# Masks of one head pair applied by VectorE instead of TensorE, with a new order of the first half, in an attention-and-MLP kernel

## Chip, cores and metric

The kernel runs on one core of a Trainium2 chip. The metric is the device time of one execution in microseconds (us), the median of several runs.

## What is computed

Attention over 4 batches, 8 heads, 768 tokens and 64 columns a head, followed by a two-layer MLP over all 3,072 tokens:

```python
scores = scale * np.matmul(q, k.transpose(0, 1, 3, 2))
stream_keep = causal & (is_sink | in_win)
mask = np.where(retr, causal, stream_keep)
scores = np.where(mask, scores, -1e9)
a = softmax(scores)
x = (a @ v), heads side by side            # 3072 x 512
h = x @ w_in                               # 512 x 2048
g = np.maximum(h, 0) + alpha * np.minimum(h, 0)
out = g @ w_out                            # 2048 x 512
```

Heads 0, 2 and 6 are "retrieval" heads with a causal mask. Heads 1, 3, 4, 5 and 7 are "streaming" heads: a token sees the first 4 tokens (sinks) and the last 64.

## The kernel before

**Segments.** The work of attention is cut into 16 segments n, four a batch. A segment is a pair of heads: (2, 6), (1, 5), (0, 4), (3, 7). Segment 3 is the fourth pair of batch 0; both of its heads are streaming. Inputs are read in fp32 into rings of four buffers each (`qf`, `kf`, `vf`), cast to bf16, transposed on TensorE (PE) for the first eight segments and by DMA later, and multiplied to scores with keys on the partitions. ScalarE (ACT) takes the exponential out of PSUM into `eR` (retrieval heads, 2 buffers) or `eS` (streaming heads, 3 buffers). A matmul with the values and a column of ones gives outputs and row sums; VectorE (DVE) divides. The result is transposed into `xT`, the MLP's input.

**Masks, two ways.** For n < 4 the mask is added on PE before the exponential: after each score matmul a second matmul of the identity with a constant of 0 and -30000 (`nmr` causal, `nms` and `nms6` streaming) goes into the same PSUM columns (lines 459 and 498). For n >= 4 the mask is multiplied in after the exponential: DVE multiplies the bf16 result by a constant of 0 and 1 (`mr`, `ms`, `ms5`; lines 476 and 527).

**MLP.** It runs in 8 pieces t of 512 or 256 tokens. `P{t}.{f}` are the matmuls with w_in (line 598), ACT takes relu(-h) (`p`, line 603), DVE makes g from it (`g`, line 610), `O{t}.{s}.{u}` are the matmuls with w_out (line 618), ACT copies the result (`o`) and POOL's or SP's queue stores it. The piece P0.f is cut in three parts (pairs 0 and 1, pair 2, pair 3) for f < 6, so that it can start before pair 3 is ready. Weights are loaded by POOL's queue with a cast: `wi0`..`wi7` for w_in (wi0 and wi1 serve columns 0 to 511, i.e. f 0 to 3; wi2 and wi3 f 4 to 7; wi4 and wi5 f 8 to 11; wi6 and wi7 f 12 to 15) and `wo0`..`wo3` for w_out (wo u serves quarter u of each O).

**The order.** All of it is one list of names, `ORDER`, written out (lines 14 to 71). Each engine gets its own instructions in the order in which their names stand in the list, and works through them one by one; waits between engines follow from the data. The names:

- `Lq n`, `Lk n`, `Lv n`: loads, issued by SP's queue (part of Lk0 and `La`, the slopes, by ACT's). A load into a ring slot waits until the slot's last reader is done. SP's loads take turns on 8 semaphores.
- `Cq n`, `Ck n.h`, `Cv n`: casts, by POOL for n <= 5 (Cq0.0 DVE, Ck0.0 ACT), by DVE later (Cq6 and Cq7 by ACT). Cv also copies the sink rows of streaming heads on POOL (line 310).
- `Tq`, `Tk`: transposes on PE; `tq` copies the result out on ACT (tq0.1 on DVE); `tk` on DVE for n < 4, on ACT later.
- `S n.h.m`: scores; `s`: exponential (ACT); `m`: mask product (DVE); `A n.h`: output matmul, `a`: its division (DVE); `X n`: transpose of the output, `x`: copy into `xT` (DVE).
- `kz, vz, sz, qz, ro, so, vo`: constants set by DVE (kz2 by ACT, kz3 by POOL); `ms`, `mr`: the 0/1 masks, made by DVE; `nms`, `nmr`: made by POOL; `warm`: filler matmuls.

PSUM has eight banks. For n < 4 scores take a pair of banks out of two pairs (0, 1) and (2, 3), transposes bank 4 or 5, outputs bank 6 or 7; later all take any bank. From n = 4 on, scores are collected and issued in a group; a group with at least 576 columns in each head is issued with the two heads on the two halves of the array (line 427), another one on the whole array (line 420).

The pieces of code that choose the way of masking:

```python
# line 495, scores of a streaming head before the late segments
                one_score(n, hh, m, sc[:, x, o:o + w], kt[:, 128 * j:128 * (j + 1)],
                          qt[:, 124 * j:124 * j + w], n >= 4)
                if n < 4:
                    nc.tensor.matmul(sc[:, x, o:o + w], ident, (nms6 if j == 6 else nms)[:, 0:w],
                                     start=False, stop=True)
# line 787, in the list of items
                if n >= 4:
                    item(f"m{n}.{hh}.{m}", M_retr if RETR[h] else M_stream, n, hh, m)
```

The functions concerned: `M_retr` (470), `M_stream` (523), `S_retr` (442), `S_stream` (483), `thirds` (480: for n < 4, m = 0 covers two thirds of 384 columns, m = 1 the last third), `emit_burst` (414), `load_w_in` (704), `cast_v` (345), `factors` (659).

Of the kernel before, what the change touches and what calls it, by code (L numbers as in the profile page):

```python
# [14 lines left out]
Lq0.0 zero La id qz nmr Lk0 kz1 sz2 kz2 Ck0.1 vo Lk1 nms Ck0.0 qz0 Lq0.1 Lq1 kz0 Cq0.0 warm0 Tq0.0 warm1 sz1 tq0.0 Lq2  # L15
vz0 Cq0.1 Tk0.0 warm2 tk0.0 Lk2 S0.0.0 sz0 s0.0.0 Tk0.1 S0.0.2 Lv0 vz1 Cq1 s0.0.2 Lk3 tk0.1 Tq0.1 S0.0.1 Ck1.0 s0.0.1
Tq1 Ck1.1 vz2 Ck2.0 Tk1 ro Cq2 tq1 tq0.1 vz3 S0.1.1 S0.1.2 Ck2.1 s0.1.1 S0.1.0 Tk2 tk1.0 Cv0 tk1.1 s0.1.2 S1.1.1 Tq2
s1.1.1 so Ck3.1 A0.0 Lv1 s0.1.0 S1.0.1 tk2.1 S1.1.0 tq2 idf tk2.0 kz3 Lv2 Ck3.0 Lq3 A0.1 Cv1 s1.0.1 wi0 m6.0.2 s1.1.0
a0.0 S1.0.0 Tk3 S2.0.2 wi1 s1.0.0 Lv3 Cq3 a0.1 Lk4 X0 tk3.0 s2.0.2 wi2 Cv2 A1.0 S2.1.0 s2.1.0 x0 A1.1 a1.0 Cv3 S2.1.1
a1.1 Tq3 s2.1.1 S2.0.1 Ck4.0 X1 tk3.1 Lq5 tq3 S2.0.0 Ck4.1 A2.1 Lk5 mr m4.0.2 s2.0.1 s2.0.0 S3.1.0 x1 A2.0 S3.1.1  # L20
s3.1.0 a2.1 s3.1.1 S3.0.0 wi3 A3.1 wi4 s3.0.0 S3.0.1 s3.0.1 a2.0 Lk6 Tk4 Lq6 X2 a3.1 x2 A3.0 P0.3.0 tk4.0 P0.2.0 Al
a3.0 X3 Ck5.0 Cq5 x3 P0.0.0 tk4.1 wi5 wi7 P0.0.1 P0.2.1 P0.3.1 P0.1.0 Tq5 al Lq4 wi6 P0.2.2 P0.1.1 Lq7 P0.3.2 P0.1.2
P1.0 ms P0.0.2 p0.3 P0.5.0 P1.6 g0.3 tq5 Ck6.1 p0.1 P1.4 P0.5.1 Ck5.1 P0.5.2 p0.0 g0.0 Lk7 g0.1 p1.6 g1.6 p0.2 P0.6
P0.4.0 Tk5 Lv5 p0.5 wo0 g0.2 one P0.4.1 g0.5 p1.0 p1.4 Cq4 g1.0 p0.6 P0.11 Ck6.0 Lq8 P0.4.2 P1.2 g0.6 wo2 tk5.0 nr
tk5.1 nz0 g1.4 p1.2 Tq4 P1.8 m10.0.2 P0.10 S5.1.2 g1.2 wo1 p1.8 kfz0 p0.4 g1.8 Lk8 kfz1 wo3 p0.11 P0.14 g0.4 Cq6 P0.13
tq4 p0.14 kfz3 p0.10 P0.9 P0.8 g0.11 p0.13 g0.14 Tq6 p0.9 g0.10 g0.13 P1.10 g0.9 P0.12 tq6 p0.8 g0.8 Cq7 p0.12 P0.7
p1.10 P1.14 S5.1.1 p0.7 s5.1.2 g0.12 O0.0.0 S4.1.1 S4.1.4 Lv4 p1.14 Lq9 S4.0.0 g1.10 s5.1.1 S5.0.0 g0.7 g1.14 S4.0.1
kfz2 s4.0.0 s4.1.1 P0.15 s4.0.1 m4.0.0 Ck7.1 m5.1.1 P1.12 m4.1.1 s4.1.4 S4.0.4 S5.1.0 p0.15 g0.15 s5.0.0 S4.1.3 S4.0.2
O0.0.1 s4.1.3 s4.0.2 S5.0.2 S4.1.2 Tk6 Cv5 m5.1.2 p1.12 O0.1.0 Cv4 s5.0.2 m4.1.3 Lk9 m5.0.0 Cq8 Ck7.0 O0.1.1 O0.1.2
s4.0.4 s4.1.2 tk6.1 tk6.0 s5.1.0 Ck8 m4.0.4 O0.0.2 S4.1.5 S4.0.5 S4.0.3 S4.1.0 S6.1.2 m5.0.2 m4.1.4 s4.0.3 s4.1.0  # L30
s4.1.5 m5.1.0 O0.1.3 s6.1.2 g1.12 m4.0.1 Tq7 S5.0.1 O0.0.3 A5.1 s4.0.5 O0.3.0 O0.3.1 o0.0 Tk7 m4.0.3 m4.1.5 a5.1
s5.0.1 m4.0.5 m4.1.0 tk7.0 O0.3.2 A4.0 m5.0.1 o0.1 A4.1 tk7.1 Lv6 a4.0 Dk8.1 Dq8 tq7 a4.1 O0.3.3 o0.3 A5.0 a5.0 Lv7
S6.0.5 S6.1.1 S7.1.1 S6.0.4 S6.1.0 S7.0.0 s7.0.0 Cq9 Cv6 s6.1.0 O1.1.0 s6.0.4 s6.1.1 S7.0.1 S6.0.3 X5 nz1 O0.2.0
m6.0.4 s6.0.5 s7.0.1 S7.1.2 S6.0.1 x5 O1.1.1 s6.0.1 Ck9 s7.1.1 O1.1.2 S6.0.2 S8.1.0 m6.0.1 s7.1.2 S7.1.0 m7.0.0 s6.0.3
S7.0.2 S6.0.0 m6.1.2 S8.1.5 O0.2.1 O0.2.2 Dq9 m6.1.1 m6.0.3 Dk9.0 s6.0.2 m7.0.1 m7.1.1 s6.0.0 s7.1.0 Dk8.0 m6.1.0
m6.0.5 s7.0.2 m7.0.2 Cv7 m6.0.0 A6.1 O0.2.3 A6.0 O1.1.3 m7.1.2 Dk9.1 ns s8.1.0 m7.1.0 Lk10 o0.2 Lq13 o1.1 a6.0 A7.1
A7.0 O1.0.0 Lv8 a6.1 S8.1.4 s8.1.4 O1.0.1 s8.1.5 S8.0.0 S8.0.3 S9.1.0 S8.1.1 a7.0 S8.1.3 a7.1 S9.0.1 Lk11 Lk12 S9.0.0
O1.0.2 s8.0.0 Ck10 X6 s8.1.3 s8.0.3 s9.0.0 s8.1.1 Lv9 Lq10 s9.0.1 m8.0.0 X4 s9.1.0 O1.0.3 X7 S8.0.1 S8.0.4 x4 S9.0.2
# [24 lines left out]
A15.0 p5.0 a15.0 p5.4 O4.1.1 g5.8 O4.0.0 a14.0 m4.1.2 O4.2.0 g5.4 X15 P5.10 O4.1.2 O4.0.1 O4.2.1 m8.0.2 x15 X14 O4.0.2
P6.8 P6.6 O4.0.3 p5.10 g5.0 P6.1 O4.3.3 O4.2.2 g5.10 P6.7 p6.8 o4.0 p6.7 p6.6 P7.6 g6.7 g6.8 O4.2.3 P6.10 O4.1.3 P6.3
p6.10 o4.3 g6.10 P7.4 o4.2 O5.1.0 O5.1.1 P7.0 p6.1 g6.6 P6.2 g6.1 p6.3 O5.0.0 g6.3 o4.1 P6.13 p6.13 P7.14 g6.13 O5.0.1
p6.2 p7.0 P6.0 g6.2 O5.1.2 P6.5 g7.0 P6.11 p6.0 g6.0 O5.0.2 p6.11 O5.1.3 p7.4 p6.5 g6.11 P7.10 p7.14 m8.1.2 o5.1 g6.5
m12.1.2 P6.9 P6.4 g7.4 p6.9 g6.9 p6.4 O5.0.3 g7.14 P7.2 O6.1.0 P6.15 g6.4 p7.2 P7.12 p6.15 O6.1.1 O6.1.2 g7.2 o5.0
O6.0.0 g6.15 P6.14 P6.12 O6.0.1 p6.14 O7.0.0 O6.0.2 g6.14 p7.6 p7.12 p6.12 g6.12 g7.6 O6.3.0 O6.2.0 O6.2.1 O6.0.3 P7.8
O6.2.2 O6.1.3 g7.12 O6.3.1 p7.8 o6.1 p7.10 O6.3.2 O6.3.3 g7.8 O7.0.1 o6.3 g7.10 o6.0 L0 O6.2.3 O7.0.2 o6.2 O7.0.3 L1
l0 L2 o7.0 l1 l2  # L70
""".split()


@with_exitstack
def kernel(
    ctx: ExitStack,
    tc: tile.TileContext,
    q: bass.AP,
    k: bass.AP,
    v: bass.AP,  # L80
    is_retrieval: bass.AP,
# [16 lines left out]
    RETR = [1, 0, 1, 0, 0, 0, 1, 0]  # L98
    PAIRS = [(2, 6), (1, 5), (0, 4), (3, 7)]
    NSINK = 4  # L100
    NT = 7
    SLOT = 256
    LAY = 8
    XD = (0, 1, 2)
    CROSS = 8

    class Tiles:

        def __init__(self, starts, masked):
            self.QS, self.RM = starts, masked  # L110
# [328 lines left out]
    def r_parts(n, m):  # L439
        return range(2 * m, 2 * m + 2) if n < 4 else [m]  # L440
# [416 lines left out]
```

## Time and profile before

| what | value |
|---|---|
| median of 5 runs | 233.09 us (231.09 to 233.79) |
| profiled execution, its own time | 233.4 us |
| its span, first to last instruction | 231.7 us |
| granted TensorE clock | 1.00 |
| first matmul with w_in | 28.59 us |
| w_in pieces landed | 25.45, 28.24, 30.01, 33.32, 35.90, 38.81 (wi5), 40.44 (wi7), 42.50 us (wi6) |
| w_out pieces landed (wo0, wo2, wo1, wo3) | 45.85, 49.23, 52.52, 55.95 us |
| first matmul with w_out | 50.77 us |

In a profile, L598 is line 598 of the kernel before. PE is TensorE's matmuls, PEld its weight loads. A group's duration of a matmul contains the way through the array, so matmuls overlap: what one costs in a full stream is the step from one start to the next. A wait is put down to the engine, line and releaser that ended last.

### The profile page before, as it was taken

How to read it: one execution, taken by the hardware profiler on the slowest of the kernel's cores; microseconds unless marked ns; L12 is line 12 of the kernel's file. 1: busy time of each engine (PE TensorE's matmuls, PEld its weight loads, DVE VectorE, ACT ScalarE, POOL GpSimd, SP SyncE). 2: the span in 40 equal slices, each digit the busy share in tenths (PEclk: the TensorE clock that was granted, in tenths of full speed). 3: DMA queues.
4: the chain of work that ended last, by engine and by line, in shares of the span. 5: the costliest groups of instructions: out<-in, count | busy, mean ns of one | idle time of the engine just before them, and what ended most of it. 6: DMA issues, size and time to landing. Idle time of an engine off the chain costs nothing.

```text
span 231.7 us, 5226 instructions
## 1 busy us (share of the span) xinstructions
PE 222.4 (96%) x1983; PEld 137.9 (60%) x2011; DVE 154.8 (67%) x395; ACT 140.1 (60%) x280; POOL 46.9 (20%) x95
## 2 busy tenths in 40 slices
PE   7899999999999999999999999999999999999993
PEld 6788855565565666575566546556854555554553
DVE  5779759996558756999997377978890335645200
ACT  6687838899868488555856764589312423623231
POOL 4759475403113530000001000010000020000000
PEclk9999999999999999999999999999999999999999
DMA  6989999999999999998789998770310130110034
GB/s 209 305 185 250 250 284 239 201 196 206 207 228 183 193 266 233 203 162 181 111 155 195 254 179 176 144 202 0 73 35 0 48 136 0 47 48 0 0 135 140
DMA packets 90834, 36.25 MB, mean 156 GB/s; under 512 B 77864, under 2 KB 89016, under 8 KB 90808
## 3 DMA queue, kind: packets, MB, share of 16 engines
q1 hardware_dynamic: 84616, 26.59, 55.0%
q0 software_dynamic: 5728, 8.91, 16.9%
q10 hardware_dynamic: 464, 0.40, 0.5%
q8 instruction: 16, 0.26, 0.5%
q14 instruction: 10, 0.08, 0.1%
HBM read 27.55 MB, written 6.29 MB: 146 GB/s over the span
## 4 chain that ended last, share of the span: by engine, by line
PE 77%; DMA 6%; ACT 4%; SPq 4%; DVE 3%; issue 2%; POOL 2%; POOLq 0%; ACTq 0%
PE P L618 34%; PE P L598 29%; PE P L553 5%; DMA w_in_b<-in_moe_w_in_dram 4%; PE P L427 4%; DVE g L610 3%; SPq L224 2%; DMA kf<-in_k_dram 2%; ACT neg L603 2%; PE P L420 2%; PE P L637 2%; PE P L578 1%; ACT qT L367 1%; DVE natm L332 1%; PE P L362 1%
## 5 line engine op out<-in xcount | busy, mean ns | idle before, releaser
L610 DVE SCALAR_TENSOR_TENSOR g<-neg,oma,P 128x512 bf16<-128x512 f32 (+1 forms) x128 | 71.9, 608 | 37.1 <-ACT neg L603 36.4
L598 PE MATMUL P<-xT,w_in_b 128*128 128x256 bf16 (+1 forms) x501 | 89.8, 325 | 1.4 <-DMA w_in_b<-in_moe_w_in_dram 0.5
L603 ACT ACTIVATE neg<-P 128x512 f32<-128x512 f32 x96 | 54.5, 605 | 60.1 <-PE P L598 51.0
L618 PE MATMUL P<-w_out_b,g 128*128 128x512 bf16 x351 | 86.4, 379 | 1.1 <-issue 0.3
L598 PEld LDWEIGHTS <-w_in_b 128*128 128x128 bf16 x512 | 48.9, 98 | 34.4 <-issue 1.8
L618 PEld LDWEIGHTS <-g 128*128 128x128 bf16 x368 | 34.0, 98 | 35.1 <-issue 1.2
L466 ACT ACTIVATE eR<-P 128x448 bf16<-128x448 f32 (+6 forms) x63 | 36.2, 621 | 7.9 <-PE P L459 2.5
L628 POOL DMA_DIRECT2D out_dram<-ot x18 | 10.1, 562 | 123.0 <-ACT ot L624 123.0
L564 DVE TENSOR_TENSOR xn<-P,rcp 128x448 bf16<-128x448 f32 (+1 forms) x32 | 19.4, 608 | 1.1
L624 ACT COPY ot<-P 128x512 f32<-128x512 f32 x23 | 13.3, 591 | 8.9 <-PE P L618 6.3
L514 ACT ACTIVATE eS<-P 128x352 bf16<-128x352 f32 x30 | 13.7, 481 | 3.5 <-PE P L420 2.3
L520 ACT ACTIVATE eS<-P 128x384 bf16<-128x384 f32 (+1 forms) x25 | 13.7, 572 | 3.2 <-PE P L498 2.8
L410 PE MATMUL P<-qT,kT 128*128 128x192 bf16 (+14 forms) x68 | 11.3, 251 | 1.3 <-DVE qT L367 0.7
L563 DVE RECIPROCAL rcp<-P 128x7 f32<-128x7 f32 (+1 forms) x32 | 6.3, 197 | 8.0 <-PE P L553 7.9
L553 PEld LDWEIGHTS <-eS 128*128 128x128 bf16 x260 | 10.3, 97 | 1.9
L553 PE MATMUL P<-vb,eS 128*128 128x65 bf16 x260 | 10.9, 193 | 0.0
L553 PEld LDWEIGHTS <-eR 128*128 128x128 bf16 x276 | 9.7, 97 | 1.5 <-ACT eR L466 0.2
L553 PE MATMUL P<-vb,eR 128*128 128x65 bf16 x276 | 10.1, 193 | 0.0
L427 PE MATMUL P<-qT,kT 64*128 64x176 bf16 (+14 forms) x151 | 9.8, 251 | 0.2
L529 DVE TENSOR_TENSOR eS<-eS,ms_near 128x352 bf16<-128x352 bf16 x30 | 9.6, 334 | 0.2
L347 POOL CAST vb<-vf 128x896 bf16<-128x896 f32 x6 | 5.9, 991 | 17.4 <-DMA vf<-in_v_dram 17.4
L427 PEld LDWEIGHTS <-kT 64*128 64x128 bf16 x151 | 6.3, 94 | 5.2 <-issue 4.7
(99 smaller groups left out, 191.0 us busy)
## 6 DMA issues: line engine op xcount, KB each, us to landing
out_dram<-ot POOLq DMA_DIRECT2D x18, 256.0 KB, 3.2
vf<-in_v_dram SPq DMA_DIRECT2D x22, 192.0 KB
kf<-in_k_dram SPq DMA_DIRECT2D x21, 192.0 KB
qf<-in_q_dram SPq DMA_DIRECT2D x18, 192.0 KB
qf<-in_q_dram SPq DMA_DIRECT2D x7, 384.0 KB
w_in_b<-in_moe_w_in_dram POOLq DMA_DIRECT2D x8, 256.0 KB, 8.9
w_out_b<-in_moe_w_out_dram POOLq DMA_DIRECT2D x4, 512.0 KB, 11.9
kf<-in_k_dram SPq DMA_DIRECT2D x9, 196.0 KB
```

The costliest lines, as they stand in the source:

```text
L410: nc.tensor.matmul(to, keys, queries, start=True, stop=stop)
L427: nc.tensor.matmul(to, keys[own], queries[own], start=True, stop=True)
L466: nc.scalar.activation(ebuf[n, hh][:, lo:hi].rearrange("p (x c) -> p x c", x=len(parts)), P[:, got[0]:got[0] + len(parts), 0:(hi - lo) // ...
L514: nc.scalar.activation(slots, sc[:, 0:352].rearrange("p (s c) -> p s c", c=176), AF.Exp, scale=scale)
L520: nc.scalar.activation(slots, sc.rearrange("p x (s c) -> p x s c", c=192), AF.Exp, scale=scale)
L553: nc.tensor.matmul(pav[:, i, :], e[:, o:o + 128], vv[:, j, hh, 0:D + 1], start=(m == 0), stop=(m == len(terms) - 1))
L564: nc.vector.tensor_tensor(xn[n][:, 0:nt, D * hh:D * hh + D], pav[:, :, 0:D], rcp.to_broadcast([128, nt, D]), op=ALU.mult)
L598: nc.tensor.matmul(psg[:, w * i:w * (i + 1)], w_in_b[:, c, 128 * fb:128 * (fb + 1)], xT[:, c, o:o + w], start=(x == 0), stop=(x == 3))
L603: nc.scalar.activation(neg[t, f], bank(held["P", t, f][0]), AF.Relu, scale=-1.0)
L610: nc.vector.scalar_tensor_tensor(g_buf[t % 2][:, fb, 0:w], neg[t, f][:, c], oma[:, fb:fb + 1], bank(got[0])[:, c], op0=ALU.mult, op1=ALU.add)
L618: nc.tensor.matmul(bank(held["O", t, s][0]), g_buf[t % 2][:, f, 128 * s:128 * (s + 1)], w_out_b[:, f, :], start=(f == 0), stop=(f == 15))
L624: nc.scalar.copy(ot, bank(got[0]))
```

## The change

For segment 3, the mask matmuls of the identity with `nms`/`nms6` fall away, and DVE multiplies the bf16 exponentials by `ms` or `ms5` afterwards, in four new items m3.0.0, m3.0.1, m3.1.0, m3.1.1 (for m = 0 over two thirds at once, 128 x 768; for m = 1 over 128 x 384). Scores of segment 3 are still issued one by one and take pairs of banks as before. The first 515 names of the list are put in another order (519 with the new ones); from S8.0.5 on the list is the same. Code, complete:

```diff
+    PEM = 3
...
-                    masked = n < 4 and a < y
+                    masked = n < PEM and a < y
...
-            if RB[m] < RO[j] + RM[j] <= RB[m + 1]:
+            if RB[r_parts(n, m)[0]] < RO[j] + RM[j] <= RB[r_parts(n, m)[-1] + 1]:
...
-                          qt[:, 124 * j:124 * j + w], n >= 4)
-                if n < 4:
+                          qt[:, 124 * j:124 * j + w], n >= PEM)
+                if n < PEM:
...
-            factor = (ms5 if m == 2 else ms).unsqueeze(1).to_broadcast([128, 1, 2, 192])
+            x = thirds(n, m)
+            factor = (ms5 if x[-1] == 2 else ms).unsqueeze(1).to_broadcast([128, len(x), 2, 192])
...
-                if n >= 4:
+                if n >= PEM:
                     item(f"m{n}.{hh}.{m}", M_retr if RETR[h] else M_stream, n, hh, m)
```

The order, up to about the last w_out quarter of the first piece:

```diff
-Lq0.0 zero La id qz nmr Lk0 kz1 sz2 kz2 Ck0.1 vo Lk1 nms Ck0.0 qz0 Lq0.1 Lq1 kz0 Cq0.0 warm0 Tq0.0 warm1 sz1 tq0.0 Lq2
-vz0 Cq0.1 Tk0.0 warm2 tk0.0 Lk2 S0.0.0 sz0 s0.0.0 Tk0.1 S0.0.2 Lv0 vz1 Cq1 s0.0.2 Lk3 tk0.1 Tq0.1 S0.0.1 Ck1.0 s0.0.1
-Tq1 Ck1.1 vz2 Ck2.0 Tk1 ro Cq2 tq1 tq0.1 vz3 S0.1.1 S0.1.2 Ck2.1 s0.1.1 S0.1.0 Tk2 tk1.0 Cv0 tk1.1 s0.1.2 S1.1.1 Tq2
-s1.1.1 so Ck3.1 A0.0 Lv1 s0.1.0 S1.0.1 tk2.1 S1.1.0 tq2 idf tk2.0 kz3 Lv2 Ck3.0 Lq3 A0.1 Cv1 s1.0.1 wi0 m6.0.2 s1.1.0
-a0.0 S1.0.0 Tk3 S2.0.2 wi1 s1.0.0 Lv3 Cq3 a0.1 Lk4 X0 tk3.0 s2.0.2 wi2 Cv2 A1.0 S2.1.0 s2.1.0 x0 A1.1 a1.0 Cv3 S2.1.1
-a1.1 Tq3 s2.1.1 S2.0.1 Ck4.0 X1 tk3.1 Lq5 tq3 S2.0.0 Ck4.1 A2.1 Lk5 mr m4.0.2 s2.0.1 s2.0.0 S3.1.0 x1 A2.0 S3.1.1
-s3.1.0 a2.1 s3.1.1 S3.0.0 wi3 A3.1 wi4 s3.0.0 S3.0.1 s3.0.1 a2.0 Lk6 Tk4 Lq6 X2 a3.1 x2 A3.0 P0.3.0 tk4.0 P0.2.0 Al
-a3.0 X3 Ck5.0 Cq5 x3 P0.0.0 tk4.1 wi5 wi7 P0.0.1 P0.2.1 P0.3.1 P0.1.0 Tq5 al Lq4 wi6 P0.2.2 P0.1.1 Lq7 P0.3.2 P0.1.2
-P1.0 ms P0.0.2 p0.3 P0.5.0 P1.6 g0.3 tq5 Ck6.1 p0.1 P1.4 P0.5.1 Ck5.1 P0.5.2 p0.0 g0.0 Lk7 g0.1 p1.6 g1.6 p0.2 P0.6
-P0.4.0 Tk5 Lv5 p0.5 wo0 g0.2 one P0.4.1 g0.5 p1.0 p1.4 Cq4 g1.0 p0.6 P0.11 Ck6.0 Lq8 P0.4.2 P1.2 g0.6 wo2 tk5.0 nr
-tk5.1 nz0 g1.4 p1.2 Tq4 P1.8 m10.0.2 P0.10 S5.1.2 g1.2 wo1 p1.8 kfz0 p0.4 g1.8 Lk8 kfz1 wo3 p0.11 P0.14 g0.4 Cq6 P0.13
...
+zero Lq0.0 id kz0 qz0 Lk0 ro nms vo kz2 nmr Ck0.1 Lq1 warm0 Lq2 Cq2 La Cq0.0 vz1 Lq0.1 Tq0.0 Lk1 Lk3 warm1 Cq0.1 Ck1.1
+Ck0.0 Tk0.0 tk0.0 warm2 tq0.0 S0.0.0 Lv0 Lk2 sz1 Tk0.1 S0.0.2 s0.0.0 Tq2 s0.0.2 Lv1 Cq1 tk0.1 vz3 Tq0.1 tq2 Ck1.0 vz0
+S0.0.1 kz1 tq0.1 vz2 qz Tq1 Tk1 Ck3.1 sz0 S0.1.1 sz2 Ck3.0 s0.0.1 kz3 tq1 s0.1.1 Ck2.0 Ck2.1 S0.1.2 tk1.0 tk1.1 S0.1.0
+Cv1 s0.1.2 S1.0.1 s1.0.1 wi0 Tk3 S1.0.0 Tk2 ms s0.1.0 Lv2 s1.0.0 S1.1.1 Lk4 tk3.0 S1.1.0 s1.1.1 tk2.1 s1.1.0 S2.1.0
+Cv0 Lq3 tk2.0 S2.0.1 Lv3 Cv2 A0.0 s2.0.1 A0.1 s2.1.0 S2.0.2 wi1 mr tk3.1 so a0.0 Lq5 A1.0 Ck4.0 Cq3 S2.1.1 Lk5 idf Tq3
+s2.0.2 a0.1 s2.1.1 A1.1 tq3 S2.0.0 s2.0.0 a1.0 wi2 A2.1 a1.1 S3.0.0 X0 S3.0.1 a2.1 s3.0.0 Ck4.1 x0 wi3 A2.0 S3.1.0
+m3.0.0 a2.0 s3.0.1 X1 s3.1.0 S3.1.1 Tk4 s3.1.1 wi5 X2 x1 P0.2.0 tk4.0 m3.0.1 Cv3 wi4 one Cq5 A3.0 m3.1.1 m3.1.0 P0.3.0
+x2 P0.0.0 A3.1 Lq4 tk4.1 a3.0 Lv4 P0.0.1 a3.1 P0.1.0 Lk6 Tq5 P0.2.1 Al P0.1.1 X3 Ck5.1 wi6 P0.3.1 P0.5.0 tq5 x3 Ck5.0
+P0.5.1 kfz0 P0.5.2 P0.6 p0.5 P0.1.2 P0.0.2 P1.0 P0.3.2 al Tk5 g0.5 p0.1 p1.0 Cq4 g0.1 p0.3 P0.4.0 P0.4.1 p0.0 g1.0
+P1.4 Lq7 g0.3 P0.4.2 P0.2.2 P1.6 tk5.0 p0.2 Lk7 p1.6 Lv6 g0.0 g0.2 p1.4 Lq6 p0.4 g1.6 wi7 P0.10 g1.4 Lv5 Tq4 P1.2 p0.6
+tk5.1 g0.6 P0.11 p0.11 tq4 g0.4 P1.8 p1.2 P0.9 g0.11 p1.8 S4.0.5 s4.0.5 p0.9 S4.1.4 P0.13 S5.1.0 g1.2 s4.1.4 s5.1.0
+P0.8 p0.13 S4.0.3 S5.1.2 g1.8 S5.1.1 S4.0.4 g0.9 s4.0.3 Lq8 p0.8 g0.13 P0.12 s5.1.1 p0.10 kfz1 P0.14 wo0 P0.7 Cv4
+P1.14 s5.1.2 Lk8 g0.8 wo1 p0.12 g0.10 g0.12 p0.14 nz1 S4.0.0 S4.0.1 Lq9 g0.14 s4.0.4 Ck7.0 p0.7 P0.15 S4.1.3 S5.0.2
+s4.0.0 s4.0.1 g0.7 p1.14 m10.0.2 S4.0.2 S4.1.2 s4.1.2 S5.0.1 nz0 O0.0.0 Cq7 g1.14 s4.0.2 s4.1.3 s5.0.1 O0.3.0 Ck6.0
+Ck7.1 wo2 s5.0.2 m4.0.3 p0.15 P1.10 O0.3.1 wo3 S5.0.0 Lk9 S4.1.1 p1.10 g1.10 g0.15 Tk7 O0.1.0 O0.1.1 Tq7 m4.0.5 O0.3.2
...
```

What POOL does in this part, in order (its instructions are taken strictly in turn):

```
before: id nmr Ck0.1 nms Cq0.1 Cq1 Ck1.0 Ck1.1 Ck2.0 Cq2 Ck2.1 Cv0 Ck3.1 kz3 Ck3.0 Cv1 wi0 wi1 Cq3 wi2 Cv2 Cv3 Ck4.0
        Ck4.1 wi3 wi4 Ck5.0 Cq5 wi5 wi7 wi6 Ck5.1 wo0 Cq4 wo2 nr nz0 wo1 kfz0 kfz1 wo3 kfz3 kfz2 Cv5 Cv4 nz1 ns
after:  id nms nmr Ck0.1 Cq2 Cq0.1 Ck1.1 Cq1 Ck1.0 Ck3.1 Ck3.0 kz3 Ck2.0 Ck2.1 Cv1 wi0 Cv0 Cv2 wi1 Ck4.0 Cq3 wi2 Ck4.1
        wi3 wi5 Cv3 wi4 Cq5 Ck5.1 wi6 Ck5.0 kfz0 Cq4 wi7 kfz1 wo0 Cv4 wo1 nz1 nz0 wo2 wo3 Cv5 kfz2 kfz3 ns nr
```

## Prediction

> **What bounds the kernel now.** I read the busy table first, then the stretches of ten microseconds, the waits of TensorE (PE), the chain that ended last, and the time lines of PE, ScalarE (ACT), VectorE (DVE) and GpSimd (POOL) over the first 60 us.
>
> ```profile
> PE 222.4 (96%) x1983; PEld 137.9 (60%) x2011; DVE 154.8 (67%) x395; ACT 140.1 (60%) x280; POOL 46.9 (20%) x95
> ```
>
> ```profile
> 0.00:10.00 10.00, 8.56 (x93) 7.50 (x94) 5.79 (x18) 6.02 (x7) 5.48 (x18) 1.00 0.83 259
> 10.00:20.00 10.00, 8.46 (x145) 7.38 (x143) 8.48 (x23) 8.01 (x11) 7.56 (x13) 1.00 0.98 217
> 20.00:30.00 10.00, 9.51 (x166) 8.18 (x166) 7.55 (x19) 7.59 (x11) 5.88 (x11) 1.00 1.14 246
> 30.00:40.00 10.00, 9.53 (x66) 5.56 (x64) 8.05 (x20) 6.45 (x13) 6.93 (x10) 1.00 1.16 264
> 40.00:50.00 10.00, 9.86 (x70) 6.14 (x70) 9.08 (x15) 9.14 (x20) 3.06 (x8) 1.00 1.22 199
> ```
>
> The second fence gives, after each stretch, the busy us of PE, weight loads, DVE, ACT and POOL, the granted clock, the DMA share and GB/s. From 30 us on PE is full, so the end comes at "start of the MLP phase + PE work left + stalls". Before 28 us no engine is full: that lead-in is a chain across engines.
>
> ```profile
> PE P L410 <- DVE qT L367: 0.7, 1, 0.7
> PE P L598 <- DMA w_in_b<-in_moe_w_in_dram: 0.5, 1, 0.5
> PE P L410 <- ACT eR L466: 0.5, 1, 0.5
> ```
>
> ```profile
> 16.64 0.94 POOL vb L347
> 17.64 0.63 POOL vb L310 x2
> 18.27 0.72 POOL w_in_b L706
> 18.98 9.26 DMA w_in_b<-in_moe_w_in_dram
> 28.24 0.35 issue
> 28.59 0.81 PE P L598 x3
> ```
>
> The first MLP matmul (28.59) waits only 0.5 us for the second piece of w_in, whose issue stood on POOL behind the cast of v1 (Cv1, 16.64). A saved microsecond on PE in the lead-in counts only if this chain moves too.
>
> **What the Trainium skill says.** (1) "TensorE: Matmul & The Clock Gate", "Wait — 56ns, not 53.3ns?": start to start is N/2.4 GHz plus about 2.5 ns, so 82.5 ns for 192 columns; the trace has 23.39, 23.47, 23.55 us: agrees. (2) "VectorE: DVE Perf Modes", "The perf-mode tier table": a bf16 tensor_tensor runs at 2x. Here 96 elements take 200 ns and 384 take 351 (L532, L527), 0.52 ns an element: agrees. (3) "TensorE: Matmul & The Clock Gate", "Architectural detail": ACT and DVE queues are strictly first in, first out. Agrees for ACT and DVE as far as the time lines tell; POOL too: a late k5 holds it for 4.24 us at 30.25 and w_in piece 5 is issued only at 31.48. (4) "DMA: Bandwidth & Descriptors", "Issuing engines are not separate DMA queues": loads issued by SP and by POOL share the same engines. The DMA share of 1.14 to 1.22 from 20 to 50 us, and 7.2 to 10.5 us from a w_in issue to its landing, agree.
>
> **The change, part by part.**
>
> *Removed on PE.* 14 mask matmuls of pair 3: ten of 192 columns, two of 148, two of 44. Start-to-start steps in the PE time line are 83, 66 and 30 ns: 10 x 0.083 + 2 x 0.066 + 2 x 0.03 = **-1.0 us**. Their durations (245 ns for 192 columns) would give 3 us, but they overlap.
>
> *Added on DVE.* Four products: two of 384 elements (351 ns, L527) and two of 768, which the trace does not show. Bounds: 0.35 us if it were no dearer than 384 elements, 0.70 as two of them; I take 351 + 384 x 0.52 = 0.55 us. Sum 1.8 us. They lie in DVE's idle time of 24 to 28 us (0.45 + 0.53 + 0.21 us of waits) and beside ACT's exps, which set that stretch. A product waits for its exp, and behind m3.0.0 on DVE stand a2.0 and x1 (the output of pair 2 and the copy that P0.2.0 needs); A3.0 and A3.1 wait for the products themselves. Uncovered they would delay the first MLP matmul by up to 1.8 us.
>
> *Moved, start.* Memsets change places and the alpha load goes behind kz2 on ACT (0.42 us of issue, beside the 1.68 us copy). Cq0.0 no longer stands behind kz1, a 64x384 memset and kz0; it waits for q0 itself, landed at 3.3 us by its semaphore. Tk0.0 follows Ck0.0 at about 5.1 us instead of 5.75, so the first score stands at about 6.8 instead of 7.46. This is lost again: q1 and q2 are now loaded ahead of k1, so k1 lands at about 9.2 us, when the old order had the same 1,920 KB in. POOL then makes Ck1.1, Cq1, Ck1.0 (0.45 + 0.8 + 0.45) until 10.9, and S0.1.1 stands at 11.3 us (11.18 before). Net 0.
>
> *Moved, middle of the lead-in.* ms (five instructions, 30.65 to 32.2: 1.5 us) comes ahead of tk3.0, tk2.1, tk2.0 on DVE (1.1 + 1.1 + 0.95). From tq0.1's end at 10.75: small memsets 0.75, tk1 2 x 1.1, ms 1.5, the three copies: tk2.0 ends at 18.4, S2.0.1 at about 19.0. Then A0.0, which needs Cv0. Before, Cv0 ran at 12.38. Now POOL has Cv1, wi0, Cv0 in this order, and v1 stands behind the same loads as before, so it lands at about 16.4: 16.4 + 0.95 + 0.63 (two sink copies) + 0.75 (issue) + 0.93 = **19.7 us**, bounds 18.8 (v1 0.9 earlier, DVE then binds at 19.0) and 20.7. PE waits 0.7 us and goes on at 19.75. ACT follows: from A0.0's end at 20.4 it has ten instructions before the MLP phase (s2.0.1 to s3.1.1 with tq3; 0.87, 0.75 or 0.42 each, tq3 0.72), 6.9 us, to 27.3. Then S3.1.1, Tk4, X2 and the copy x1 let P0.2.0 start at about **28.15**. The old start was 28.59, but then A3.0 and A3.1 (0.39 us each) were done; now they follow. So the MLP phase stands at 28.15 + 0.78 = 28.93: **+0.3 us** net, the -1.0 included; the re-ordering itself costs 1.3.
>
> *Moved weight loads.* POOL order by the same sums: wi0 18.0, wi1 21.0 (behind Cv0, Cv2), wi2 23.0, wi3 24.1, wi5 24.7, wi4 27, wi6 about 33 (behind Ck5.1), wi7 about 36 (behind Cq4). wi1 alone in its queue lands at about 26.5 to 28 (9.26 us as before would be 30): in time for 28.15, barely. wi2/wi3 are wanted by P0.5.0 4.2 us of PE work later, 32.4, and land at about 31.5; wi6/wi7 are wanted by P0.13 at about 43.6 and land at about 43. Each has under 1 us to spare; I put down **+0.3 us** for what is not covered (0 to 1.5; below 0 is possible by 0.6, the PE gap at 38.13 where wi5 landed at 38.81).
>
> *Bursts.* Scores from pair 4 on are issued in groups; a group with 576 columns in each head runs both heads side by side. Counting groups from the two orders with columns/2.4 GHz and 0.19 us for entering and leaving the 64-row form (gaps of 0.10 + 0.095 in the PE time line): 7.3 us before, 7.1 now: **-0.2**.
>
> Sum: +0.3 + 0.3 - 0.2 = +0.4 us on the span of 231.7, so 232.1. That execution took 233.4 us, the median of five is 233.09 (231.09 to 233.79); the change goes on the median: **233.5 us**.
>
> **Rivals.** *The saving goes through.* The old PE waits (0.7 and 0.5 us by line, some 6 us of bare PE in the lead-in) leave room, and if v1 lands 2 us earlier with less in front of Cv0's chain, the re-ordering costs 0 to 0.3 instead of 1.3: -1.0 - 0.2 - the 0.5 for w_in = 231.4 to 232; with the gap at 38.13 gone as well, 230.8. For it: wi3, wi4, wi5 no longer wait behind Cq5 and Ck5.0, which cost POOL 4.24 us. Against it: nothing in the new order lets Cv0 run before v1.
>
> *Slower: w_out waits for v4.* Cv4 now stands on POOL between wo0 and wo1. v4's rows are packets of 256 B on the queue that shares engines with the weights, and in the old trace v5 took from about 36 to 55 us (POOL waits 12.71 us for it). Here v4 can be in at about 44 only because wo0 runs out then; wo1 is issued at 45.5 and lands 6 to 12 us later (w_out's old issue to landing: 11.9 us median), 51.5 to 57, wo2 and wo3 at 55 to 60. PE wants wo1 (O0.3.1) at about 54 and wo2 at 57.7. It decides when v4 lands after about 46: each us later is a us of PE stall; at 49, +3 us, 236.5. For it: the 12.71 us wait. Against it: w_in traffic ends sooner now.
>
> *The removed matmuls were cover.* If PE merely idles where the masks were, for ACT's exps, the saving is nothing from the first and the end is +1.0 worse than where the masks bound: this is part of my likeliest case and its upper edge, 234.5.
>
> **How the numbers follow.** Likeliest, the saving is used up by the later Cv0 and MLP start: 0.50, 233.5, own range 232.3 to 234.8. Saving through: 0.27, 231.6, from 230.0. Weights late: 0.23, 236, from 234.5 to 238.5. Leaving out about a tenth at each side gives 231.0 to 236.5. Over 1% is 2.3 us (about what a measurement of this kernel can tell from no change): faster means under 230.8, not quite half of the second case, 0.13; slower means over 235.4, most of the third, 0.19; the rest is 0.68.
>
> **What would show it.** Right: no L498 matmul past pair 2, four L527-line products at 25 to 29 us; A0.0's matmuls start right after Cv0's cast, at 19 to 20.5 us; first MLP matmul at 27.6 to 28.8 with A3 behind it; PE full from 30 us on. Wrong: A0.0 long before 19 us, or the first MLP matmul under 27.3 (then the second case); a PE wait of over 1 us for w_in at 32 or 43 us, or for w_out at 54 to 60 (then the third); or a DVE wait for k7 at Ck7.0 with g0.7 and a PSUM bank behind it, which I have not priced apart.

## The result, and the profile after

| | before | changed |
|---|---|---|
| median | 233.42 us, 80 runs (231.09 to 236.36) | 234.27 us, 43 runs (233.37 to 235.76) |
| ratio to before | 1 | 1.006 (1.0045 to 1.0075) |
| profiled execution: time, span | 233.4, 231.7 us | 234.55, 232.8 us |
| A0.0 | 14.40 us | 19.96 us |
| wi1 issued, landed | 18.98, 28.24 us | 21.27, 30.38 us |
| first matmul with w_in | 28.59 us | 30.73 us |
| S8.0.5, from where the two orders are the same | 89.58 us | 91.38 us |

There is no gain: by the ratio the changed kernel is 0.6% slower, inside the 1% that was called no change. The ratio compares only executions within 1.5% of their kernel's fastest, which leaves out slow ones of the kernel before and none of the changed one; the medians over all executions, in the table, differ by 0.85 us, or 0.36%. The busy times of the stretches of ten microseconds come first, columns as in the prediction (PE, weight loads, DVE, ACT, POOL, clock, DMA share, GB/s).

```profile
10.00:20.00 10.00, 7.68 (x90) 5.89 (x88) 9.46 (x26) 7.29 (x10) 7.74 (x14) 1.00 0.99 238
20.00:30.00 10.00, 8.19 (x173) 7.42 (x172) 8.18 (x24) 7.20 (x11) 8.93 (x15) 1.00 1.16 233
30.00:40.00 10.00, 9.22 (x87) 6.09 (x90) 6.59 (x14) 5.09 (x9) 3.89 (x8) 1.00 1.21 208
```

Before, PE was busy for 8.46, 9.51 and 9.53 us in these. The holes are at 10 to 30 us, in the lead-in. The longest waits of PE behind its warm-up, by line, releaser, total us, times and longest:

```profile
PE P L363 <- POOL g L320: 1.3, 2, 0.9
PE P L555 <- DVE xn L566: 1.2, 1, 1.2
PE P L600 <- DMA w_in_b<-in_moe_w_in_dram: 1.0, 1, 1.0
```

The wait for w_in is 1.0 us where it was 0.5, though it begins later. The chain of work that ended last, in the same stretch as the prediction showed of before:

```profile
17.95 0.30 POOL vb L311
18.25 0.72 POOL w_in_b L708
18.97 0.00 issue
18.97 1.95 POOL vb L348 x2
20.92 0.05 issue
20.97 0.29 POOL vb L311
21.27 9.11 DMA w_in_b<-in_moe_w_in_dram
30.38 0.35 issue
30.73 0.38 PE P L600
```

Before, wi1 followed wi0 at once (18.27, 18.98). Now two casts of v stand between them (Cv0 and Cv2, 1.95 us) with a sink copy, so wi1 is issued 2.29 us later, takes 9.11 us as it took 9.26, and the MLP begins 2.14 us later. Just below this chain lies a second one. DVE's time line (start, duration, line, operation; in brackets the idle time ahead of it):

```profile
22.52 0.30 DVE L293 MEMSET eS<- 128x288 f32 x1 [1.25 <-ACT eS L521]
22.84 0.20 DVE L565 RECIPROCAL rcp<-P 128x6 f32<-128x6 f32 x1
...
27.50 0.56 DVE L529 TENSOR_TENSOR eS<-eS,ms 128x768 bf16<-128x768 bf16 x1
...
29.41 0.35 DVE L529 TENSOR_TENSOR eS<-eS,ms 128x384 bf16<-128x384 bf16 x1
```

and PE's, for what waits behind the first two:

```profile
23.69 0.55 PE L555 MATMUL P<-vb,eS 128*128 128x65 bf16 x13 [1.20 <-DVE xn L566]
...
30.73 0.38 PE L600 MATMUL P<-xT,w_in_b 128*128 128x512 bf16 x1 [0.98 <-DMA w_in_b<-in_moe_w_in_dram]
```

The memset `so` waits 1.25 us for an exponential, with the division a0.0 behind it; A1.0 needs the bank that a0.0 frees, and PE waits 1.20 us. From the first w_in matmul to S8.0.5 the changed kernel needs 60.65 us, the one before 60.99, and here A3.0 and A3.1 (0.39 us each) lie inside that stretch, before they did not: 1.1 us less for the same work. The two ends of that stretch, before and changed:

```profile
89.58 0.36 PE L420 MATMUL P<-qT,kT 128*128 128x64 bf16 x3
...
91.38 0.36 PE L421 MATMUL P<-qT,kT 128*128 128x64 bf16 x3
```

One gap of before is gone:

```profile
38.90 0.81 PE L598 MATMUL P<-xT,w_in_b 128*128 128x512 bf16 x3 [0.39 <-ACT neg L603]
```

(Before, one matmul stands at 38.13 and the next at 38.90, right behind wi5, which lands at 38.81; the row names ACT, whose instruction had ended at 38.58. Now wi5 lands at 35.47 and PE runs through.)

### The profile page after: what moved, and what is told of

Read it like the earlier page. It is cut to its first block, busy times and chain, and to the rows that moved or that the text cites. A ratio compares the mean times of both kernels' runs of the same rounds, so it can differ in the third digit from the quotient of the medians.

```text
span 232.8 us, 5200 instructions
## 1 busy us (share of the span) xinstructions
PE 221.6 (95%) x1968; PEld 136.8 (59%) x1997; DVE 156.1 (67%) x399; ACT 139.7 (60%) x280; POOL 48.1 (21%) x95
## 4 chain that ended last, share of the span: by engine, by line
PE 85%; DMA 9%; POOL 2%; issue 1%; DVE 1%; ACT 0%; POOLq 0%
PE P L600 36%; PE P L620 34%; PE P L555 6%; DMA kf<-in_k_dram 4%; DMA w_in_b<-in_moe_w_in_dram 4%; PE P L428 4%; PE P L421 2%; PE P L639 2%; PE P L363 1%; DMA vf<-in_v_dram 1%; PE P L580 1%; POOL vb L348 1%; DVE kT L390 1%; POOL g L320 0%; POOL w_in_b L708 0%
## 5 line engine op out<-in xcount | busy, mean ns | idle before, releaser
L612 DVE SCALAR_TENSOR_TENSOR g<-neg,oma,P 128x512 bf16<-128x512 f32 (+1 forms) x128 | 72.8, 609 | 43.2 <-ACT neg L605 42.2
L605 ACT ACTIVATE neg<-P 128x512 f32<-128x512 f32 x96 | 55.4, 617 | 57.9 <-PE P L600 50.4
L467 ACT ACTIVATE eR<-P 128x448 bf16<-128x448 f32 (+6 forms) x63 | 37.7, 633 | 9.6 <-PE P L428 3.8
L411 PE MATMUL P<-qT,kT 128*128 128x192 bf16 (+13 forms) x68 | 10.6, 250 | 1.6 <-ACT eR L467 1.0
L428 PE MATMUL P<-qT,kT 64*128 64x176 bf16 (+18 forms) x154 | 9.8, 250 | 0.1
```

Source lines behind the costliest of these rows:

```text
L411: nc.tensor.matmul(to, keys, queries, start=True, stop=stop)
L428: nc.tensor.matmul(to, keys[own], queries[own], start=True, stop=True)
L467: nc.scalar.activation(ebuf[n, hh][:, lo:hi].rearrange("p (x c) -> p x c", x=len(parts)), P[:, got[0]:got[0] + len(parts), 0:(hi - lo) // ...
L605: nc.scalar.activation(neg[t, f], bank(held["P", t, f][0]), AF.Relu, scale=-1.0)
L612: nc.vector.scalar_tensor_tensor(g_buf[t % 2][:, fb, 0:w], neg[t, f][:, c], oma[:, fb:fb + 1], bank(got[0])[:, c], op0=ALU.mult, op1=ALU.add)
```

## The experiments

Theory at the start: the loss is made in the lead-in, by wi1's late issue, with the `so` stall and the late Cv0 just under it; the mask saving is hidden behind the wait for wi1; and the second part of the order gives some time back. Rivals: the products on DVE cost the time; w_out or another weight is late; the order costs nothing and the masks' removal gives nothing. Two landmarks serve as marks: the first w_in matmul, and S8.0.5, ahead of which every kernel here has done the same PE work (but for the mask matmuls). Ratios are to the kernel before on the same chip. Orders are edited by moving names; a line of a diff is one name.

**The order alone (order_only).**

```diff
-    PEM = 3
+    PEM = 4
```

> The changed kernel's order with the masks of segment 3 still added by TensorE (the four m3 products left out of the list). Theory (second w_in piece bounds): TensorE gets 1.0 us more to do but stood ready 1.2 us before the piece landed at 30.38, so the first w_in matmul stays at 30.6 to 31.0 us and the time stays that of the changed kernel, 1.003 to 1.008 of before. Rival (the masks count in full): first w_in matmul about 31.6, 1.009 to 1.012 of before.

235.33 us, 1.0077 (1.0048 to 1.0106), from six executions. wi1 lands at 30.23, the first w_in matmul is at 30.58 (30.73 in the changed kernel). PE's time line of this kernel:

```profile
29.87 0.55 PE L579 MATMUL P<-ident,xn 128*128 128x128 bf16 x7
30.58 0.38 PE L599 MATMUL P<-xT,w_in_b 128*128 128x512 bf16 x1 [0.16 <-issue]
```

The group at 29.87 starts its last transpose at 30.20; in the changed kernel that is at 29.52. So the masks' removal makes PE ready 0.68 us sooner, and PE then waits 0.98 us for wi1: the saving is spent there. At S8.0.5 nothing is left of it (91.23 us here, 91.38 in the changed kernel). The order alone brings the whole loss (1.0077 and 1.006 have overlapping intervals), so the products on DVE are not its cause.

**The masks alone (masks_only).** The order of before, with the changed code:

```diff
+ms
 so
...
 a2.1
+m3.1.0
...
 s3.1.1
+m3.1.1
...
 s3.0.0
+m3.0.0
...
 s3.0.1
+m3.0.1
 a2.0
...
-ms
```

> The old order with the masks of segment 3 moved to VectorE (four products put in behind their exponentials, the making of ms moved ahead of the memset so). Theory (w_in piece wi1 bounds, landed at 28.24 before): TensorE is ready about 1 us earlier and waits about 1.2 to 1.5 us for the same piece; first w_in matmul at 28.4 to 28.8 us, 0.998 to 1.001 of before. Rival (the masks count): first w_in matmul at 27.6, 0.995 to 0.997 of before.

234.44 us, 1.0036 (1.0012 to 1.0061). DVE's time line:

```profile
26.01 0.56 DVE L529 TENSOR_TENSOR eS<-eS,ms 128x768 bf16<-128x768 bf16 x1 [0.36 <-ACT eS L521]
26.77 0.36 DVE L529 TENSOR_TENSOR eS<-eS,ms 128x384 bf16<-128x384 bf16 x1 [0.20 <-ACT eS L521]
27.04 0.20 DVE L565 RECIPROCAL rcp<-P 128x7 f32<-128x7 f32 x1
```

The products wait for their exponentials with a2.0 (27.04) queued behind them; X2 needs a2.0, and PE waits 1.41 us for it. wi1 had landed at 26.56; the first w_in matmul is at 29.61. What the prediction called uncovered, "up to 1.8 us", is real when a product stands in front of a2.0. So neither expectation came true: the first w_in matmul was set neither by wi1 nor by the time that the masks took on PE, but by the place of the products.

**The same with the products behind a2.0 (old_masks2).** a2.0 directly behind m3.1.0, ahead of the other three products; A3.0 behind P0.3.0, X3 and x3 behind P0.0.0.

> The old order with the masks of segment 3 on VectorE, as in the earlier run with the masks alone, but a2.0 ahead of three of the four products and the first w_in matmuls ahead of A3.0. Theory (in the earlier run the products stood in front of a2.0 and X2 waited 1.4 us for it): that wait is gone, the first w_in matmul stands at 26.9 to 28.6 depending on when wi1 lands, 0.995 to 0.999 of before. Rival (products on VectorE cost more than the placement): no better than the earlier run, 1.002 to 1.005.

233.52 us, 0.9989 (0.9968 to 1.001). wi1 lands at 27.41, the first w_in matmul is at 27.65, 0.94 us before that of before, but with A3.0 still to do and waits of 0.57 and 0.59 us for m3 and a3 around it:

```profile
26.59 0.33 PE L555 MATMUL P<-vb,eS 128*128 128x65 bf16 x5 [0.57 <-DVE eS L529]
...
27.65 0.59 PE L600 MATMUL P<-xT,w_in_b 128*128 128x512 bf16 x2
28.83 0.55 PE L555 MATMUL P<-vb,eS 128*128 128x65 bf16 x13 [0.59 <-DVE xn L566]
```

S8.0.5 is at 89.52, where before has 89.58. The lead of 0.94 us is spent on A3.0 (0.39 us) and on the second of these waits (0.59). The marks and the ratio are inside what the theory said.

**wi1 ahead of Cv2 (wi1_up), in the changed kernel.**

```diff
+wi1
 Cv2
...
-wi1
```

> The changed kernel with one item moved on GpSimd: wi1 ahead of the cast Cv2 (still behind Cv0). Theory: wi1 is issued at about 19.9 instead of 21.27 and lands at about 29; TensorE, ready at 29.5 with so's stall kept, then starts w_in at 29.4 to 29.8 instead of 30.73; 1.000 to 1.004 of before. Rival (the piece's landing is set by the traffic and not by its issue): landing still above 30, no change.

234.45 us, 1.0048 (1.0027 to 1.007). wi1 is issued at 19.93, lands at 29.19:

```profile
29.27 0.55 PE L580 MATMUL P<-ident,xn 128*128 128x128 bf16 x7
29.66 0.59 PE L600 MATMUL P<-xT,w_in_b 128*128 128x512 bf16 x2
```

The wait for w_in is gone, the first w_in matmul is 1.07 us earlier, P2.5 and S8.0.5 0.85 us earlier, the span of this execution 0.8 us shorter. The ratio does not show it: 0.85 us less than the changed kernel's would be about 1.0024, and the interval begins at 1.0027. That wi1 set the start is shown; that this start is worth its 0.85 us over many executions is not.

**`so` early (so_early), in the changed kernel.**

```diff
 sz2
+so
...
-so
```

> The changed kernel with one item moved: the memset so ahead of the first exponential of a streaming head. Theory (two waits in series, the later one sets the start): TensorE is ready about 1.0 to 1.3 us earlier, at 28.3 to 28.6, but wi1 is still issued at about 21.3 and lands at about 30.3, so the first w_in matmul stays at 30.5 to 30.8 and the time at 1.003 to 1.007 of before. Rival (so's stall alone sets the start): first w_in matmul at 29.4 to 29.7, 0.999 to 1.003.

234.29 us, 1.0048 (1.0023 to 1.0072). The 1.20 us wait of A1.0 is gone, and comes back nearly whole ahead of the first w_in matmul:

```profile
28.41 0.55 PE L580 MATMUL P<-ident,xn 128*128 128x128 bf16 x7
30.91 0.59 PE L600 MATMUL P<-xT,w_in_b 128*128 128x512 bf16 x2 [1.94 <-DMA w_in_b<-in_moe_w_in_dram]
```

S8.0.5 is at 91.78, no earlier than in the changed kernel. A stall beside the one that binds is worth nothing alone here.

**Cv0 ahead of Cv1, wi1 right behind wi0 (w_early); the same with `so` early (w_so_early).**

```diff
+Cv0
 Cv1
 wi0
+wi1
...
-Cv0
...
-wi1
```

> The changed kernel with two items moved on GpSimd: Cv0 ahead of Cv1 (into its idle time before v1 lands) and wi1 right behind wi0. Theory: wi1 is issued at about 19.0 instead of 21.27 and lands at 28.0 to 28.5; TensorE then is ready last, at about 29.4, so the first w_in matmul stands at 29.0 to 29.6 instead of 30.73, and the time at 0.999 to 1.003 of before. Rival (something else late, as the DVE copy x1 or ACT's exponentials, or the order after it): no gain over the changed kernel, 1.004 to 1.008.

> As w_early, and the memset so moved ahead of the first exponential of a streaming head, so that VectorE does not wait 1.25 us for an exponential with a0.0 behind it (A1.0 waited 1.2 us for the bank that a0.0 frees). Theory (two causes in series: w_in piece, then so): first w_in matmul at 27.9 to 28.7 us with the products A3 behind it, 0.993 to 0.998 of before. Rival (so was only an apparent cause, ACT's chain from A0.0 on sets the pace): same as w_early, 29.0 to 29.6.

w_early: 234.44 us, 1.0042 (1.0021 to 1.0063), wi1 landed at 29.74 and TensorE ready last, first w_in matmul at 31.17. w_so_early: 233.74 us, 1.0029 (1.0008 to 1.005), first w_in matmul at 29.96. From A0.0 to the first w_in matmul takes 9.85 us in the first and 8.82 in the second: once wi1 does not bind, the `so` stall does, and without that stall PE waits again for wi1, by 0.40 us (landed at 29.61). Both profiled executions had a stretch at half clock (below), so their landmarks are late by it. The theory of neither came true: w_early gained nothing clear over the changed kernel, as its rival said, and w_so_early gained about half of the loss (1.0029 against 1.006, with intervals that still touch), not the whole and more.

**More of the lead-in mended (lead_all).** w_so_early, and besides Cv0 further up behind kz3, A0.0 behind S1.0.0, A0.1 behind S1.1.0.

> The changed kernel with its lead-in mended in four places: Cv0 cast behind kz3, in GpSimd's idle time; A0.0 and A0.1 moved up to S1.0.0 and S1.1.0, into TensorE's waits for score banks; so ahead of the streaming exponentials; wi1 right behind wi0. Theory (the order lost its time in Cv0, so and wi1): ACT no longer waits for A0.0, the first w_in matmul stands at 27.6 to 28.6 us and the time at 0.990 to 0.997 of before. Rival (the loss is also in the order from the MLP on): 0.999 to 1.004 with the first w_in matmul just as early.

234.23 us, 1.0031 (1.0007 to 1.0054). A0.0 runs at 16.57 (19.96), but PE then waits 1.08 us for ACT at 21.61, and wi1 lands at 29.30 and sets the first w_in matmul at 29.43. S8.0.5 is at 90.30, 1.08 us better than in the changed kernel, 0.72 short of before. These edits together win back more than half of the loss at this mark, but neither the theory's time nor its start was reached. Part of the rest is wi1 once more: PE waits 0.58 us for it. It is issued 0.59 us later than before (19.57 against 18.98) and takes 9.73 us instead of 9.26.

**The old lead-in with the second part of the new order (hyb_pe, hyb_dve).** The names up to P0.3.0 of before (of old_masks2 in hyb_dve), then the other names in the changed kernel's order.

> The order of the kernel before up to P0.3.0, masks of pair 3 on TensorE as before, and from there the order of the changed kernel. Theory (the new order loses in the lead-in and gives back about 1 us between the first w_in matmul and P2.5): first matmul with w_in at 28.4 to 28.8 us, P2.5 at 85.8 to 86.4 us against 86.98 before, ratio 0.994 to 0.998. Rival (the shorter stretch in the changed kernel was only slack that a later start leaves to the loads): a wait for a piece of w_in comes back at 32 to 40 us, P2.5 at 86.8 to 87.4 us, ratio 0.999 to 1.002.

> The lead-in of the kernel before, masks of pair 3 on VectorE with the products behind the division of pair 2's output, and from P0.3.0 on the order of the changed kernel. Theory: first matmul with w_in at 27.4 to 28.4 us, P2.5 at 85.4 to 86.4 us, ratio 0.991 to 0.997 (both savings together, and faster than the kernel with this lead-in and the old second part, 0.999). Rival (the second part of the new order is worth nothing with an early start): P2.5 at 86.7 to 87.3 us, ratio 0.997 to 1.001.

236.73 us, 1.0177 (1.0116 to 1.0237, six executions), and 235.22 us, 1.0082 (1.0049 to 1.0114): slower than both the theory and the rival said. In hyb_pe a wait for w_in between 32 and 40 us came back, as the rival had it (wi3 lands at 34.22):

```profile
34.35 3.41 PE L599 MATMUL P<-xT,w_in_b 128*128 128x512 bf16 x19 [1.66 <-DMA w_in_b<-in_moe_w_in_dram]
```

A second stop begins on POOL, in the time line of the same kernel:

```profile
40.29 0.82 POOL L319 CAST natq<-qf 128x768 bf16<-128x768 f32 x1 [7.26 <-DMA qf<-in_q_dram]
41.05 0.61 POOL L707 DMA_DIRECT2D w_in_b<-in_moe_w_in_dram  x1
```

In the new order wi7 stands behind Cq4 on POOL, and q4 is loaded ahead of k6 and q6. The old lead-in issues k6 and q6 first; q4 is cast at 40.29 instead of 31.82, wi7 goes out at 41.05 instead of 32.58 and lands at 47.48, and PE stops for it:

```profile
47.62 1.02 PE L599 MATMUL P<-xT,w_in_b 128*128 128x512 bf16 x4 [1.60 <-DVE g L611]
```

(The row names g as the releaser; wi7 landed 0.14 us before the matmul started.) The two halves of an order are tied by their loads.

**The same with the loads mended (hyb3_copy), and its control (old3_copy).** q4, v4, k6, q6 in the changed kernel's sequence, wi3, Cv3, wi5 ahead of wi4; old3_copy is old_masks2. Both leave out the transposes by DMA of segments 8 to 15 and of their outputs: plain copies of the same tiles stand in their place, so neither computes the outputs of the task, and their times are compared with each other. Code, the same in both:

```diff
-                          natq[n].rearrange("p i c -> p (i c)"), transpose=True)
+                          natq[n])
...
-                          natk[n][:, 896 * hh:896 * hh + 128 * nt], transpose=True)
+                          natk[n][:, 896 * hh:896 * hh + 128 * nt].rearrange("p (i r) -> p i r", r=128))
...
-        nc.sync.dma_start(xT[:, heads(n)[0], o:o + nt * r].rearrange("p (i r) -> p i r", r=r),
-                          xn[n][0:r, 0:nt].rearrange("p i c -> p (i c)"), transpose=True)
+        nc.sync.dma_start(xT[0:r, heads(n)[0], o:o + nt * r].rearrange("p (i r) -> p i r", r=r),
+                          xn[n][0:r, 0:nt, 0:r])
```

> Leaves out the transposes by DMA of segments 8 to 15 and of their outputs: plain copies of the same tiles stand in their place, about 60 us and later. Otherwise the kernel with the old order and masks on VectorE. Both theories: first matmul with w_in at 27.5 to 28.8 us, P2.5 at 86.6 to 87.6 us, as with the transposes (27.65, 86.92); it is the control for the other kernel of this call, and its ratio to the kernel before means little by itself.

> Leaves out the same transposes by DMA, with plain copies instead. The lead-in of the old order with masks on VectorE up to P0.3.0, then the changed kernel's order; and now also the loads q4, v4, k6, q6 and the pieces of w_in (wi3 and wi5 ahead of wi4, Cv3 between them) in the changed kernel's sequence, so that Cq4 does not hold wi7 on POOL. Theory (the second part of the new order saves about 1 us over the old one): q4 cast by 33 us, wi7 issued by 34 us, no wait of TensorE over 0.5 us between 30 and 50 us, P2.5 0.7 to 1.5 us earlier than in the control, ratio lower than the control's by 0.003 to 0.006. Rival (with an early start the second part is worth nothing): P2.5 within 0.4 us of the control's, ratio within 0.002 of it, or worse. If wi7 is still issued after 38 us, neither is tested.

old3_copy 233.6 us, 1.0034 (1.001 to 1.0058); hyb3_copy 234.3 us, 1.0034 (1.0007 to 1.0061). In hyb3_copy q4 is cast at 33.77, wi7 issued at 34.53, and PE has no wait over 0.5 us between 30 and 50 us: the pairing now works. P2.5 is at 86.12, 0.80 us ahead of old_masks2's 86.92, which looks like the theory, but P2.5 was a poor mark: in the new order a burst of 0.68 us comes behind it that the old order has ahead of it. S8.0.5 is at 89.49, old_masks2's at 89.52 (the control's own execution had a half-clock stretch). By time and by mark the pairing as a whole gains nothing.

That does not make the second part worth nothing. hyb3_copy's time line of PE:

```profile
26.16 0.34 PE L555 MATMUL P<-vb,eS 128*128 128x65 bf16 x6 [0.26 <-POOL vb L311]
...
28.29 0.59 PE L600 MATMUL P<-xT,w_in_b 128*128 128x512 bf16 x2
```

Its first w_in matmul stands 0.64 us behind old_masks2's 27.65, with the same PE work ahead of it: Cv3 now stands behind wi3 on POOL, and PE waits 0.26 us for v3's sink rows and 0.73 instead of 0.57 us for a product. From there to S8.0.5 it needs 61.20 us, old_masks2 61.87 for the same work. And the seven kernels with the lead-in and the second part of the new order (changed, order_only, wi1_up, so_early, w_early, w_so_early, lead_all) need 60.65 to 60.87 us for that stretch, whether it begins at 29.43 or at 31.17. So no run here shows that the changed kernel's shorter MLP phase came from its late start; the marks speak for the order, by about 0.7 us in this pair of single executions, and the mended loads cost as much in the lead-in.

## Why the prediction was right

It said 233.5 us (231.0 to 236.5) and no measurable change; 234.27 came, and the likeliest case (the saving used up by a later MLP start) is the one that happened. But what made the start late was the landing of wi1, not the chain from Cv0 over ACT that the sum followed, so one of the signs of being right did not come: the first MLP matmul stood at 30.73, not at 27.6 to 28.8 (and the four products at 27.5 to 31.1, not at 25 to 29). By its steps:

- *Masks off PE, -1.0 us.* The removal made PE ready 0.68 us sooner than the order alone did (29.52 against 30.20). Right in kind, and right that it counts only if wi1's chain moves: it was spent on the wait for wi1.
- *Products, 0.55 and 0.35 us.* Measured 0.56 and 0.35. Hidden in the changed kernel, as said; masks_only shows the price where one stands ahead of a2.0 (1.41 us of PE).
- *Start, net 0.* S0.1.1 came at 12.34, not 11.3: PE waited 0.94 us for POOL's cast Cq1 ahead of it. The first score came at 7.34, not 6.8. Wrong by 1 us, but absorbed, since A0.0 could not run before Cv0, and Cv0 ended at 19.9.
- *Middle.* Cv0's end was put at 19.7 and A0.0 at 19.75; A0.0 ran at 19.96. Right. From there to a ready PE the sum said 28.15; PE's last start ahead of the w_in matmuls was 29.52. The missing term is `so`: the prediction counted `ms` and the three copies on DVE, but not this memset ahead of a0.0, which cost 1.2 us.
- *wi1.* This is the step that was wrong by most: "wi1 alone in its queue lands at about 26.5 to 28 (9.26 us as before would be 30): in time for 28.15, barely." The issue was right (21.0, measured 21.27), the landing 30.38: 9.11 us, just what before had shown. The duration measured in the same trace stood in the text, in brackets, and was set aside for a shorter one that no row supported. The first w_in matmul was 2.6 us later than predicted for it.
- *Weights later on, +0.3 us.* No wait for w_in from wi2 on; none for w_out. wi3 landed at 33.77, later than the 31.5 put down, but PE came later too; wi6 and wi7 were issued 3 us earlier than put down (30.07 and 32.58) and had landed by 40.86. With the gap at 38.13 gone this term was below nothing, within the bound named (by 0.6).
- *Bursts, -0.2 us.* Not measured apart; they are inside the 1.1 us that the MLP phase was shorter.
- *Rivals.* v4 held w_out on POOL as described (8.14 us of waiting) but was cast at 42.25, below the point of 46 from which it decides, and PE never waited. The saving did not go through: A0.0 ran at 19.96, not long before 19. Both were refuted by the marks named for them. Of the third, that the masks were cover, a part is so: of the 1.0 us taken off PE 0.68 us arrived as an earlier PE, and none at S8.0.5.

That the number came out this close is partly luck. The start was 2.6 us later than in the sum; the MLP phase up to S8.0.5 was 1.1 us shorter where the sum had it 0.1 longer (+0.3 - 0.2); and behind S8.0.5, where the order is the same, this execution was 0.7 us faster than that of before, which no step foresaw. From 0.4 us these make the 1.1 measured on the span; the medians differ by 0.85.

What stays open: lead_all keeps 0.3% after all its edits. The ratio and the medians differ by up to 0.3% between themselves (old3_copy: 1.0034, but 1.0003 by the medians 233.6 and 233.54), so the variants' places among each other are not resolved at this size. And S8.0.5 to the end, same names in the same order, took 142.1 us before, 141.4 in the changed kernel and 142.3 in order_only: single executions differ by as much as the effects here, and which part of the 1.80 us at S8.0.5 survives to the median can't be read from one. No version here beats the kernel before: old_masks2 (0.9989) is level with it.

## What to carry to other kernels

Follow the first weight piece that the next phase needs to the queue that issues it, and price its landing by the duration that the trace shows, however empty its queue will be. When one wait binds, look for the waits within a microsecond below it: removing the first or the second alone moves a mark and not the time. Two halves of a hand-written order can't be joined without their loads; compare them at a mark behind which the same work is left, and look at what each has already spent when the second half begins.

## What was not expected of the hardware

**A half-clock stretch in the lead-in of some executions.** The granted clock falls to a half for 3.4 us: at 11.68 to 15.1 us in w_early, 12.07 to 15.5 in w_so_early, 11.47 to 14.89 in old3_copy, 28.99 to 32.4 in masks_only. PE's time line of w_early, the same 128 columns in the stretch and after it:

```profile
14.72 0.31 PE L460 MATMUL P<-nmr,ident 128*128 128x128 bf16 x1
...
15.20 0.22 PE L460 MATMUL P<-nmr,ident 128*128 128x128 bf16 x1
```

A mean clock of 0.99 marks such an execution. It was in 9 of 191 executions of the kernel before that were recorded beside the experiments and in 9 of 44 of the changed kernel, where PE is busy for 7.68 instead of 8.46 us from 10 to 20 us; they took 0.9 and 0.8 us more in the median (234.32 against 233.39; 235.01 against 234.19). It costs less elsewhere: in so_early it was in 10 of 22, at 0.2 us. A share of 20% instead of 5%, at 0.85 us, is about 0.13 us of mean difference; without them the medians still differ by 0.8 us. The Trainium skill ("TensorE: Matmul & The Clock Gate", "What's actually happening") has a free-running window of 3413 ns and a clock of either full or half speed, set by how busy PE was: length and halves agree; that idle time in the lead-in is the cause here is argued, not shown, and where in the span the stretch lay is known for the profiled executions alone.

**A w_in piece took 5.8 to 11.4 us to land in the runs here, close behind another piece or not.** wi1 took 9.11 us in the changed kernel, where it was issued 3.07 us after wi0, 9.26 in the kernel before, 0.76 us after wi0, as much in wi1_up and 9.73 in lead_all. Issued at about the same time (19.21 and 19.00) in the same order, it took 8.20 us in old_masks2 and 9.96 in old3_copy, whose execution had the half-clock stretch: the landing alone varies by more than a microsecond between executions.
